# Copies of down-sampled rows issued from ScalarE's queue in two groups, ahead of and behind one block of exponentials

## The chip, the core and the metric

The kernel runs on one core of a Trainium2 chip. The metric is the device time of one execution in microseconds (us). The engines are TensorE (PE; its weight loads are PEld), VectorE (DVE), ScalarE (ACT), GpSimd (POOL) and SyncE (SP), which here only issues transfers. Each engine works through its own instructions in the order in which they were built; a transfer is issued as an instruction of SP, ACT or POOL and lands later by itself, carried by 16 DMA engines that all queues share.

## The reference, cut to what matters

An attention block, and two gated layers behind it. `q`, `k`, `v` have 4 batches, 8 heads, 576 positions and 64 features.

```
q_d, k_d, v_d = means of 4 neighbouring positions          # 144 rows for each head
out_up = repeat(softmax(q_d k_d^T / 8) v_d, 4)             # the down-sampled part
out_local = softmax over |i - j| < 4 of (q k^T / 8) v      # the local part
x = out_up + out_local                                     # 2304 tokens x 512
x = (silu(x w_gate) * (x w_val)) w_out                     # 512 -> 1536 -> 512
out = (h * clip(h + 3, 0, 6) / 6) w2_out,  h = x w2_in     # 512 -> 2048 -> 512
```

All is float32 in accuracy; the inputs come as float64, whose words the kernel decodes itself.

## The kernel before

The 2304 tokens go through the two layers in five blocks (`BLOCKS`, in units of 64 tokens). For every block the weights are brought in pairs of units `w`, split into a high and a low part `wr` (L263 on ACT, L268 on DVE), and multiplied: `pG` (gate) and `pV` (value) of L357, `aO` (output) of L1034, `pH` and `aP` for the second layer. In the first block the weights are decoded from the raw words (`top`, L236 on ACT; `w`, L245 on DVE) and stored in a scratch of the device memory (`kept`, L251, issued by ACT); later blocks read them there. `pG`, `pV` and `pH` use two PSUM banks in turn (`mm`): G0, G1, V0, V1, G2, G3, so G3 writes the bank that V1 wrote, which is free when DVE has multiplied V1 into `sl` (L1004). `gV` is that product, split again (L1009, L1010).

The first batch's attention comes ahead of all this, in `first_batch`, whose steps stand in the string `FRONT`, one word for a step; each engine runs its share of them in this order. The local part works on tiles of 96 positions, i from 0 to 5: `SC` scores, `M` maxima, `W` exponentials (ACT), `N` normalisation (DVE), `PT` transposes into PSUM, `Pa` and `Pd` copies out of it into `turned` (ACT and DVE), `V` the product with the values (`fO` in the traces), `Xh` and `Xl` the result as high and low parts `xr`. `turned` has room for two tiles, so the next `Pa` into the same half waits for the `V` that reads it. The down-sampled part is `dS`, `dM`, `dE`, `dT`, `dP`, `dO`, `dN`; its result lies in `odN`, a piece of a tile named `tmp`. To add it, the values of tile i, `vw[i]`, have 24 more rows under their 102 (WK to KR), and `turned` has ones for them; the step `od` copies 24 rows of `odN` under each of the six tiles by a transfer within the on-chip memory (`join_od`), and `V` of tile i waits for its copy. `de` and `to` decode weights, `hi` and `lo` split them, for the first units.

Two steps concern the second batch: `two` loads two of each four neighbouring positions of its `q` and `k` into staging tiles (`twoq`, `twok`, four transfers on POOL), and `sums` loads the other two on top with an addition (four accumulating transfers), then adds the two that are left (L716, `dnq`, `dnk`, on POOL). The staging tiles belong to a pool that is closed behind `first_batch`; the tiles into which SP loads the second batch's pieces of `q`, `k` and `v` (`load_chunk`, through L141) take their place, so these loads wait for the last sum. With `q` and `k` there, DVE computes the products `pr` (L839) of the second batch between its other work; its place on DVE is the scheduler's choice, as is the place of the transposes `pqT` of the sums (L336) on PE.

Every transfer counts its completion in a semaphore. There are eight for SP and ACT together (DMAHW0 to 7) and eight for POOL (DMASW0 to 7), given out in turn; a transfer whose semaphore another still uses waits for that one.

Of the kernel before, what the change touches and what calls it, by code (L numbers as in the profile page):

```python
# [46 lines left out]
Tq01 Tq00 Eq00 Eq01 Rq0 Tk00 Tk01 Ek01 Tq10 Ek00 Rk0 Tq11 Tk11 dS0 Eq10 Ek11 Eq11 Rq1 Tq20 Tk10 Eq20  # L47
Tk20 Tq21 dM0 Ek10 Ek20 Rk1 dE0 Tq31 Eq21 Tq30 Tk21 Tk31 Eq31 Tk30 dS1 Rq2 Eq30 Ek21 Ek31 Ek30 Rq3
SC0 dM1 M0 Rk3 dE1 Rk2 dT0 dP0 W0 SC1 dS3 dM3 dT1 dP1 SC2 M1 dE3 W1 dS2 dT3 N0 dM2 dP3 SC3 dE2 dT2
PT0 M2 to0 N1 M3 two dP2 to1 de0 Pd0 W3 dO0 dO3 dN0 dN3 dO2 N3 dO1 Pa0 W2 dN2 dN1 od sums to2 PT1  # L50
Pa1 Pd1 SC5 SC4 M5 W5 PT3 V1 M4 N2 Pa3 de1 Xh1 W4 V0 Xh0 Pd3 Xl1 N5 PT2 V3 Pd2 Pa2 Xl0 hi0 PT5 Xh3
N4 Pd5 Pa5 Xl3 to3 V2 Xh2 PT4 de2 Xl2 Pd4 Pa4 de3 V5 lo0 Xh5 V4 Xh4 Xl5 Xl4 hi1 to4 lo1
"""


# [1 line left out]
def tile_kernel(  # L57
# [12 lines left out]
    nc = tc.nc  # L70
# [68 lines left out]
    def late(eng, dst, src):  # L139

        tc.keep_in_program_order(eng.dma_start(dst, src))  # L141
# [172 lines left out]
    def down_sums(b, kinds, gate=None):  # L314
        if gate is not None:
            tc.keep_in_program_order(nc.gpsimd.tensor_copy(consts[:gate.shape[0], 60:61], gate))
        for ws in kinds:
            for t in range(4):
                for w in ws:
                    if t == 0:  # L320
                        dn[w] = sp.tile([NJH, 2, H, D], F32, tag="dn" + w, name=f"dn{w}{b}", bufs=1)
                    src = {"q": q, "k": k, "v": v}[w]
                    for half in range(2):
                        tok = src[b, :, half * NJH * 4:(half + 1) * NJH * 4, :].rearrange("h (j t) d -> j t h d", t=4)
                        how = {"accum_op": ALU.add} if t else {}
                        tc.keep_in_program_order(nc.gpsimd.dma_start(dn[w][:, half], tok[:, t], **how))
                    yield
# [15 lines left out]
    def down_T(b, dn, qk):  # L343
        for w in "qk":
            qk[w] = sp.tile([P, NC, NJ], F32, tag=w + "dT", name=f"{w}dT{b}", bufs=1)
        for w, hc, pt in sums_T(b):
            nc.scalar.activation(qk[w][:, 2 * hc:2 * hc + 2], pt, AF.Copy, scale=1 / 128 if w == "q" else 1.0)
            yield
# [13 lines left out]
    def first_batch():  # L362

        QT = 96
        WK = QT + 6
        KR = WK + QT // 4
# [3 lines left out]
        with tc.tile_pool(name="fp", bufs=1) as fp:  # L370
# [25 lines left out]
            odN = tmp[:NJH, NC * S:NC * S + 2 * DM].rearrange("p (g e) -> p g e", g=2)  # L396
# [53 lines left out]
            vw = []  # L450
# [17 lines left out]

            def join_od(i):
                half, j = divmod(i * QT // 4, NJH)  # L470
                late(nc.gpsimd, vw[i][WK:KR, i % 2], odN[j:j + QT // 4, half])

            for n in range(4):
                load_vd(n)
# [241 lines left out]
                            nc.gpsimd.tensor_tensor(dn[w][:, half], st[:, :, 0], st[:, :, 1], op=ALU.add)  # L716
                        )

            def od():
                for i in (1, 0, 3, 2, 5, 4):  # L720
                    join_od(i)

            def to(i):
# [9 lines left out]
            def lo(i):  # L733
# [4 lines left out]
                "dN": dN, "SC": SC, "M": M, "W": W, "N": N, "PT": PT,  # L738
                "Pa": Pa, "Pd": Pd, "V": V, "Xh": Xh, "Xl": Xl, "sums": sums, "two": two,
                "od": od, "to": to, "de": de, "hi": hi, "lo": lo,  # L740
            }
            for step in FRONT.split():
# [346 lines left out]
    for bi in range(NB):  # L1089
# [29 lines left out]
        sums = iter(())  # L1119
        if db:  # L1120
            sums = down_T(db, dn, qk)
            if bi:
                sums = chain(down_sums(db, ["qk", "v"], state["os"][:, (UMAX // 2 - 2) * DM:][:, :1]), sums)
# [69 lines left out]
```

## Time and profile before

| what | value |
|---|---|
| median of 3 runs | 959.81 us (959.5 to 960.22) |
| profiled execution | 959.29 us |
| its span, first to last instruction | 957.6 us |
| busy in the span | PE 97%, DVE 76%, ACT 53%, POOL 12% |
| TensorE's granted clock, mean | 0.99 |

Busy shares are means over stages that differ: TensorE is full in the blocks and has gaps in the first 80 us, where the first batch's attention runs. What matters there is which wait ended last. In a timeline a row has the start, the duration, the engine, the line, the operation, what it writes and reads, how many instructions it stands for, and in brackets how long the engine had been idle before it and what released it. "issue" in the chain is time in which the engine waited for nothing that the profile shows.

### The profile page before, as it was taken

How to read it: one execution, taken by the hardware profiler on the slowest of the kernel's cores; microseconds unless marked ns; L12 is line 12 of the kernel's file. 1: busy time of each engine (PE TensorE's matmuls, PEld its weight loads, DVE VectorE, ACT ScalarE, POOL GpSimd, SP SyncE). 2: the span in 40 equal slices, each digit the busy share in tenths (PEclk: the TensorE clock that was granted, in tenths of full speed). 3: DMA queues.
4: the chain of work that ended last, by engine and by line, in shares of the span. 5: the costliest groups of instructions: out<-in, count | busy, mean ns of one | idle time of the engine just before them, and what ended most of it. 6: DMA issues, size and time to landing. Idle time of an engine off the chain costs nothing.

```text
span 957.6 us, 13058 instructions
## 1 busy us (share of the span) xinstructions
PE 931.2 (97%) x4848; PEld 789.4 (82%) x4848; DVE 730.4 (76%) x1066; ACT 504.4 (53%) x942; POOL 113.7 (12%) x124
## 2 busy tenths in 40 slices
PE   8799999999899999999999999999999999999997
PEld 5677888777799978878888778888888888999996
DVE  6689967899879979999755799996347994445652
ACT  4785667876444587553334664443335444444542
POOL 7440012000063200015410000000000000000000
PEclk8999999999999999999999999999999999999999
DMA  9899899586699823359962222453223223433331
GB/s 228 178 255 369 294 334 344 166 263 208 236 285 255 159 89 110 130 180 229 216 137 88 67 67 91 165 205 101 97 90 109 89 88 116 148 133 132 120 123 33
DMA packets 100239, 161.08 MB, mean 168 GB/s; under 512 B 53488, under 2 KB 57200, under 8 KB 100176
## 3 DMA queue, kind: packets, MB, share of 16 engines
q1 hardware_dynamic: 57680, 131.43, 42.5%
q0 software_dynamic: 37600, 11.00, 10.6%
q10 hardware_dynamic: 4896, 17.83, 4.7%
q8 instruction: 38, 0.62, 0.3%
q14 instruction: 25, 0.20, 0.1%
HBM read 137.31 MB, written 22.54 MB: 167 GB/s over the span
## 4 chain that ended last, share of the span: by engine, by line
PE 77%; DVE 11%; DMA 4%; issue 3%; ACT 3%; SPq 1%; POOL 0%; ACTq 0%; DVEq 0%
PE aP L1034 17%; PE pH L357 17%; PE aO L1034 13%; PE pG L357 13%; PE pV L357 12%; DVE wr L268 3%; DVE pv L876 1%; DMA vw<-tmp 1%; PE pS L930 1%; SPq L141 1%; DMA w<-in_moe_w_gate_dram 1%; DVE xf L905 1%; DMA kept<-w 1%; PE pO L780 1%; ACT held L153 1%
## 5 line engine op out<-in xcount | busy, mean ns | idle before, releaser
L268 DVE TENSOR_TENSOR wr<-w,wr 128x1024 fp32r<-128x1024 f32 x170 | 207.6, 1222 | 117.9 <-ACT wr L263 117.7
L263 ACT ACTIVATE wr<-w 128x1024 fp32r<-128x1024 f32 x170 | 179.6, 1056 | 127.6 <-issue 61.4
L357 PE MATMUL pH<-x,wr 128*128 128x512 f32 (+1 forms) x960 | 214.0, 373 | 0.0
L1034 PE MATMUL aP<-wr,gH 128*128 128x512 f32 x864 | 212.5, 396 | 0.3 <-ACT gH L1009 0.3
L357 PEld LDWEIGHTS pH<-x,wr 128*128 128x128 f32 x960 | 173.6, 189 | 25.2 <-issue 2.7
L1034 PEld LDWEIGHTS aP<-wr,gH 128*128 128x128 f32 x864 | 159.9, 188 | 35.6 <-issue 2.7
L357 PE MATMUL pG<-xr,wr 128*128 128x512 f32 (+1 forms) x720 | 153.7, 368 | 1.7 <-ACT xr L153 1.2
L357 PE MATMUL pV<-xr,wr 128*128 128x512 f32 (+1 forms) x720 | 153.6, 368 | 0.9 <-ACT sl L998 0.9
L1034 PE MATMUL aO<-gV,wr 128*128 128x512 f32 (+1 forms) x720 | 152.7, 368 | 0.0
L357 PEld LDWEIGHTS pG<-xr,wr 128*128 128x128 f32 x720 | 130.9, 188 | 19.1 <-ACT xr L153 1.4
L357 PEld LDWEIGHTS pV<-xr,wr 128*128 128x128 f32 x720 | 130.9, 188 | 18.1 <-ACT sl L998 1.4
L1034 PEld LDWEIGHTS aO<-gV,wr 128*128 128x128 f32 x720 | 130.8, 188 | 16.7
L1007 ACT ACTIVATE h<-pH,consts 128x512 f32<-128x512 f32 (+1 forms) x80 | 51.5, 643 | 63.1 <-PE pH L357 62.6
L1009 ACT ACTIVATE gV<-sl 128x512 fp32r<-128x512 f32 (+1 forms) x60 | 35.0, 584 | 75.4 <-DVE sl L1004 75.4
L998 ACT ACTIVATE sl<-pG 128x512 f32<-128x512 f32 (+1 forms) x60 | 33.3, 554 | 67.0 <-PE pG L357 66.9
L1009 ACT ACTIVATE gH<-h 128x512 fp32r<-128x512 f32 (+1 forms) x80 | 46.9, 586 | 31.0 <-DVE h L1008 30.8
L839 DVE TENSOR_TENSOR pr<-q,k 128x1792 f32<-128x1792 f32 x27 | 54.6, 2021 | 10.1 <-DMA k<-in_k_dram 9.9
L1008 DVE SCALAR_TENSOR_TENSOR h<-h,pH 128x512 f32<-128x512 f32 (+1 forms) x80 | 50.5, 632 | 14.3 <-ACT h L1007 13.5
L236 ACT ACTIVATE top<-w 128x512 f16<-128x512 bf16 x68 | 52.8, 792 | 13.3 <-DMA w<-in_moe_w_out_dram 4.2
L1010 DVE TENSOR_TENSOR gH<-h,gH 128x512 fp32r<-128x512 f32 (+1 forms) x80 | 50.5, 633 | 11.2 <-ACT gH L1009 10.9
L876 DVE TENSOR_TENSOR pv<-sc,v 128x1792 f32<-128x1792 f32 x27 | 54.6, 2023 | 0.5
L245 DVE SCALAR_TENSOR_TENSOR w<-w,top 128x512 int32<-128x512 int32 x68 | 46.8, 702 | 10.5 <-ACT top L236 7.5
(133 smaller groups left out, 757.9 us busy)
## 6 DMA issues: line engine op xcount, KB each, us to landing
w<-kept SPq DMA_DIRECT2D x136, 512.0 KB
kept<-w ACTq DMA_DIRECT2D x34, 512.0 KB
w<-in_moe_w_out_dram SPq DMA_DIRECT2D x28, 512.0 KB
w<-in_moe_w_in_dram SPq DMA_DIRECT2D x16, 512.0 KB
w<-in_moe_w_gate_dram SPq DMA_DIRECT2D x12, 512.0 KB
w<-in_moe_w_val_dram SPq DMA_DIRECT2D x12, 512.0 KB
out_dram<-os SPq DMA_DIRECT2D x16, 256.0 KB
dnv<-in_v_dram POOLq DMA_DIRECT2D x24, 144.0 KB, 7.7
```

Of the source, the lines that this page charges most:

```text
L236: behind(nc.scalar.activation(halves(top[i % 2], 2, F16)[:, :, 1], h3.bitcast(BF16), AF.Copy))
L245: behind(nc.vector.scalar_tensor_tensor(w32[i // 2][:, i % 2].bitcast(I32), h12, 13, top[i % 2], op0=ALU.logical_shift_right, op1=ALU.bitw ...
L263: behind(nc.scalar.activation(parts[i][:, 0], w32[i // 2].rearrange("p u e -> p (u e)"), AF.Copy))
L268: behind(nc.vector.tensor_tensor(r[:, 1], s, r[:, 0].bitcast(F32), op=ALU.subtract))
L357: nc.tensor.matmul(ps, r[:, a, c], x[:, c, b_, :ps.shape[1]], start=part is HIGH and a == c == 0, stop=part is LOW and c == NC - 1,)
L839: nc.vector.tensor_tensor(pr, qt[:, a:a + SUB, None, :].to_broadcast([P, SUB, W, D]), win(kt, a, SUB), op=ALU.mult)
L876: nc.vector.tensor_tensor(pr, pe[:, a:a + SUB, :, None].to_broadcast([P, SUB, W, D]), win(vt, a, SUB), op=ALU.mult)
L1007: nc.scalar.activation(h, ps, AF.Relu, scale=1 / 6, bias=half1[:, 0:1])
L1008: nc.vector.scalar_tensor_tensor(h, h, 1.0, ps, op0=ALU.min, op1=ALU.mult)
L1009: nc.scalar.activation(g[:, 0, :nt], h, AF.Copy)
L1010: nc.vector.tensor_tensor(g[:, 1, :nt], h, g[:, 0, :nt].bitcast(F32), op=ALU.subtract)
L1034: nc.tensor.matmul(ps, **one, start=f_ == 0 and a == b_ == 0, stop=f_ == nf - 1 and b_ == 1,)
```

## The change

The step `od` becomes two, `od0` (tiles 1 and 0) and `od1` (tiles 3, 2, 5, 4). They stand in `FRONT` behind `M5`, on the two sides of `W5`, where `od` stood behind `dN1` and ahead of `sums`. The six copies are issued by ACT in place of POOL.

```diff
-PT0 M2 to0 N1 M3 two dP2 to1 de0 Pd0 W3 dO0 dO3 dN0 dN3 dO2 N3 dO1 Pa0 W2 dN2 dN1 od sums to2 PT1
-Pa1 Pd1 SC5 SC4 M5 W5 PT3 V1 M4 N2 Pa3 de1 Xh1 W4 V0 Xh0 Pd3 Xl1 N5 PT2 V3 Pd2 Pa2 Xl0 hi0 PT5 Xh3
...
+PT0 M2 to0 N1 M3 two dP2 to1 de0 Pd0 W3 dO0 dO3 dN0 dN3 dO2 N3 dO1 Pa0 W2 dN2 dN1 sums to2 PT1 Pa1
+Pd1 SC5 SC4 M5 od0 W5 od1 PT3 V1 M4 N2 Pa3 de1 Xh1 W4 V0 Xh0 Pd3 Xl1 N5 PT2 V3 Pd2 Pa2 Xl0 hi0 PT5
...
             def join_od(i):
                 half, j = divmod(i * QT // 4, NJH)
-                late(nc.gpsimd, vw[i][WK:KR, i % 2], odN[j:j + QT // 4, half])
+                late(nc.scalar, vw[i][WK:KR, i % 2], odN[j:j + QT // 4, half])
...
-            def od():
-                for i in (1, 0, 3, 2, 5, 4):
+            def od(n):
+                for i in ((1, 0), (3, 2, 5, 4))[n]:
                     join_od(i)
```

On POOL, from the second half of the plain loads on, before (what a row waits for is in brackets):

```order
L703 DMA twok_594<-in_k_dram 72x8x128 [waits DMAHW7_49,DMAHW6_49,PE_49]
L141 DMA vw_261<-tmp 24x512 [waits DVE_49]
L141 DMA vw_261<-tmp 24x512
L141 DMA vw_265<-tmp 24x512 x2
L141 DMA vw_268<-tmp 24x512 [waits DMASW0_49]
L141 DMA vw_268<-tmp 24x512 [waits DMASW1_49]
L703 DMA twoq_588<-in_q_dram 72x8x128 [waits DMASW2_49]
L703 DMA twoq_590<-in_q_dram 72x8x128 [waits DMASW3_49]
L703 DMA twok_592<-in_k_dram 72x8x128 [waits DMASW4_49]
```

and now:

```order
L703 DMA twok_594<-in_k_dram 72x8x128 [waits DMAHW7_49,DMAHW6_49,PE_49]
L703 DMA twoq_588<-in_q_dram 72x8x128 [waits DMASW0_49]
L703 DMA twoq_590<-in_q_dram 72x8x128 [waits DMASW1_49]
L703 DMA twok_592<-in_k_dram 72x8x128 [waits DMASW2_49]
L703 DMA twok_594<-in_k_dram 72x8x128 [waits DMASW3_49]
```

The four plain loads count in DMASW0 to 3. With the copies gone, each accumulating load waits for the plain load into the same tile; before, it waited for the load or copy that had the semaphore last.

On DVE, in the first block behind the first decodings, before (`sl_0`, `sl_1` belong to V0 and V1, `wr_999` to the weights of V2 and V3, `pr` to the second batch):

```order
L245 SCALAR_TENSOR_TENSOR w_8_1023<-w_8_884,top_159 128x512
L1010 TENSOR_TENSOR gV_0_991<-sl_0_942,gV_0_991 128x512
L1004 TENSOR_TENSOR sl_1_964<-sl_1_964,pV_1_1002 128x512
L268 TENSOR_TENSOR wr_999<-w_6_970,wr_999 128x1024
L839 TENSOR_TENSOR pr_0_0_1092<-q_0_972,k_0_974 128x1792
L1010 TENSOR_TENSOR gV_1_1015<-sl_1_964,gV_1_1015 128x512
L245 SCALAR_TENSOR_TENSOR w_8_1023<-w_9_890,top_161 128x512
```

and now:

```order
L839 TENSOR_TENSOR pr_0_0_1092<-q_0_972,k_0_974 128x1792
L1010 TENSOR_TENSOR gV_0_991<-sl_0_942,gV_0_991 128x512
L268 TENSOR_TENSOR wr_999<-w_6_970,wr_999 128x1024
L1004 TENSOR_TENSOR sl_1_964<-sl_1_964,pV_1_1002 128x512
L245 SCALAR_TENSOR_TENSOR w_8_1023<-w_9_890,top_161 128x512
L245 SCALAR_TENSOR_TENSOR w_10_1066<-w_10_967,top_159 128x512
```

`pr` stands ahead of `gV_0`, `wr_999` and `sl_1` in place of behind them.

On PE, in the first block from the second `pV` on, now (`pG_3` is the fourth `pG`, G3):

```order
L357 MATMUL pV_1_1002<-xr_786,wr_918 128x512 x11
L357 MATMUL pG_2_1025<-xr_786,wr_948 128x512 [waits DVE_49]
L357 MATMUL pG_2_1025<-xr_786,wr_948 128x512 x11
L336 MATMUL pqT_0_1162<-ident,dnq_684 128x72 [waits PE_49,Pool_49]
L336 MATMUL pqT_0_1162<-ident,dnq_684 128x72 [waits Pool_49]
L336 MATMUL pqT_0_1162<-ident,dnq_684 128x72 x2
L357 MATMUL pG_3_1047<-xr_786,wr_948 128x512 [waits DVE_49]
```

The order of the products is as before; the first transposes `pqT` have come from behind the first `aO` to between `pG_2` and `pG_3`.

## Rows read from the trace of the kernel before

**Rows 1.** The chain of waits: start (us), duration (us), what held it.
```profile
10.07 4.72 DMA fnk<-in_k_dram
...
37.91 9.59 DMA vw<-tmp
...
120.57 5.44 PE pG L357 x24
```

**Rows 2.** TensorE's timeline, from the last stage of the first batch on.
```profile
45.79 1.55 PE L153 MATMUL fO<-turned,vw 126*64 126x96 f32 x16 [5.78 <-DMA vw<-tmp]
...
57.77 5.78 PE L357 MATMUL pG<-xr,wr 128*128 128x512 f32 x24 [1.24 <-ACT xr L153]
...
68.83 5.60 PE L357 MATMUL pG<-xr,wr 128*128 128x512 f32 x24
...
78.08 3.03 PE L357 MATMUL pV<-xr,wr 128*128 128x512 f32 x12 [0.94 <-ACT sl L998]
```

**Rows 3.** ScalarE's timeline; ACTq is an issue of a transfer.
```profile
37.44 0.67 ACT L153 ACTIVATE turned<-fPT 102x384 f32<-102x384 f32 x1
38.41 0.34 ACT L153 ACTIVATE held<-fS,fnm 96x102 f32<-96x102 f32 x1 [0.30 <-DVE fnm L153]
...
46.81 0.49 ACT L153 ACTIVATE turned<-fPT 102x384 f32<-102x384 f32 x1 [5.69 <-PE fO L153]
...
56.80 0.33 ACTq L251 DMA_DIRECT2D kept<-w  x1
57.26 0.46 ACT L153 ACTIVATE xr<-fO 128x384 fp32r<-128x384 f32 x1
```

**Rows 4.** GpSimd's timeline.
```profile
30.76 1.87 POOL L703 DMA_DIRECT2D twoq<-in_q_dram  x2 [0.52 <-issue]
...
37.37 3.09 POOL L141 DMA_DIRECT2D vw<-tmp  x6 [3.14 <-DVE tmp L153]
43.30 1.45 POOL L703 DMA_DIRECT2D twoq<-in_q_dram  x1 [2.83 <-DMA twok<-in_k_dram]
45.12 1.40 POOL L703 DMA_DIRECT2D twoq<-in_q_dram  x1 [0.38 <-DMA twok<-in_k_dram]
46.03 3.29 POOL L703 DMA_DIRECT2D twok<-in_k_dram  x2
55.60 5.46 POOL L716 TENSOR_TENSOR dnq<-twoq 72x512 f32<-72x512 f32 x2 [6.28 <-DMA twoq<-in_q_dram]
63.95 3.07 POOL L716 TENSOR_TENSOR dnk<-twok 72x512 f32<-72x512 f32 x2 [2.88 <-DMA twok<-in_k_dram]
```

**Rows 5.** SyncE's issues of the second batch's first loads.
```profile
67.04 0.33 SPq L141 DMA_DIRECT2D q<-in_q_dram  x1
67.42 0.42 SPq L141 DMA_DIRECT2D k<-in_k_dram  x1
```

**Rows 6.** VectorE's timeline about `pr`.
```profile
73.22 2.02 DVE L839 TENSOR_TENSOR pr<-q,k 128x1792 f32<-128x1792 f32 x1 [2.38 <-DMA k<-in_k_dram]
75.17 0.69 DVE L1010 TENSOR_TENSOR gV<-sl,gV 128x512 fp32r<-128x512 f32 x1
...
78.90 1.22 DVE L268 TENSOR_TENSOR wr<-w,wr 128x1024 fp32r<-128x1024 f32 x1
80.04 0.68 DVE L1004 TENSOR_TENSOR sl<-sl,pV 128x512 f32<-128x512 f32 x1
```

**Rows 7.** What the tile `twoq` shows: its four transfers' time to landing.
```profile
DMA to landing us min/median/max: 6.5/10.1/12.3
```

**Rows 8.** Busy time by stretch: engines, then TensorE's granted clock, DMA share, GB/s.
```profile
33.00:57.00 24.00, 17.49 (x228) 15.03 (x226) 16.43 (x39) 16.43 (x72) 11.37 (x13) 0.86 1.16 211
57.00:63.00 6.00, 5.23 (x23) 4.30 (x24) 5.70 (x8) 5.59 (x8) 4.07 (x2) 1.00 1.02 337
63.00:66.00 3.00, 3.00 (x15) 2.49 (x14) 1.40 (x2) 2.26 (x4) 2.05 (x2) 1.00 0.53 105
45.80:50.60 4.80, 4.60 (x41) 3.89 (x42) 2.61 (x5) 3.70 (x19) 3.53 (x3) 0.50 1.11 251
```

More of the change, by code (lines that the diff above doesn't have):

```diff
@@ L49 @@
 SC0 dM1 M0 Rk3 dE1 Rk2 dT0 dP0 W0 SC1 dS3 dM3 dT1 dP1 SC2 M1 dE3 W1 dS2 dT3 N0 dM2 dP3 SC3 dE2 dT2
-PT0 M2 to0 N1 M3 two dP2 to1 de0 Pd0 W3 dO0 dO3 dN0 dN3 dO2 N3 dO1 Pa0 W2 dN2 dN1 od sums to2 PT1
-Pa1 Pd1 SC5 SC4 M5 W5 PT3 V1 M4 N2 Pa3 de1 Xh1 W4 V0 Xh0 Pd3 Xl1 N5 PT2 V3 Pd2 Pa2 Xl0 hi0 PT5 Xh3
-N4 Pd5 Pa5 Xl3 to3 V2 Xh2 PT4 de2 Xl2 Pd4 Pa4 de3 V5 lo0 Xh5 V4 Xh4 Xl5 Xl4 hi1 to4 lo1
+PT0 M2 to0 N1 M3 two dP2 to1 de0 Pd0 W3 dO0 dO3 dN0 dN3 dO2 N3 dO1 Pa0 W2 dN2 dN1 sums to2 PT1 Pa1
+Pd1 SC5 SC4 M5 od0 W5 od1 PT3 V1 M4 N2 Pa3 de1 Xh1 W4 V0 Xh0 Pd3 Xl1 N5 PT2 V3 Pd2 Pa2 Xl0 hi0 PT5
+Xh3 N4 Pd5 Pa5 Xl3 to3 V2 Xh2 PT4 de2 Xl2 Pd4 Pa4 de3 V5 lo0 Xh5 V4 Xh4 Xl5 Xl4 hi1 to4 lo1
 """
```

## The prediction

> **What bounds the kernel now.** I read the chain of waits first, since it names the work that sets the end. From about 78 us on it holds matmuls of TensorE almost without a gap, a run of 24 taking 5.44 us [rows 1], so the time is set by when TensorE comes through the stages before that, and an edit in the first batch is worth what it moves there. The chain names one long link in the first batch, 9.59 us of the copies `vw<-tmp` [rows 1]. TensorE's timeline shows what that link costs: a stop of 5.78 us before the first `fO`, whose matmuls read the copied rows, then the first `pG` at 57.77, the second pair of `pG` at 68.83, and one more small stop, 0.94 us, before the half pair of `pV` at 78.08 [rows 2]. The reader should compare this with the DVE rows, because that second stop has a cause that the change touches: DVE stood 2.38 us until the load of `k` landed and ran `pr` at 73.22 only then [rows 6]. SP's rows tell why `k` came so late: `q` and `k` are issued at 67.04 and 67.42 [rows 5], right behind the last sum `dnk` on GpSimd (63.95 + 3.07 = 67.02), which had itself waited for the load of `twok` [rows 4]. So there are two chains in the first 80 us: copies, `fO`, `pG`; and sums, `q` and `k`, `pr`.
>
> **The copies.** Six copy issues leave GpSimd and six come to ScalarE. Before, the first stands at 37.37, when the last normalisation is done, and the six issues take 3.09 us [rows 4]. Their landing takes 9.59 us [rows 1], although each has only 48 KB, because they stand in one queue behind four loads of 288 KB, of which POOL still saw one land at 43.30 [rows 4]. On ScalarE two copies come between `turned` (37.44) and the exponentials (38.41) [rows 3]. An issue on that queue takes 0.33 us [rows 3], so two cost 0.7 us, of which the 0.30 us that ScalarE waits there now is hidden; the exponentials start about 0.3 us late. Nobody waits for them early, and ScalarE next stands idle 5.69 us [rows 3], which takes in the four later issues (1.3 us) as well.
>
> How soon a copy lands on ScalarE's queue no row shows. Bounds: 4.72 us for a load of 144 KB on SP's queue while the DMA engines were busy [rows 1], and the 9.59 us of now. I take 4, near the first, because nothing else stands in ScalarE's queue then: `fO` starts at about 42 in place of 45.79. From the next `turned` (46.81) to the last `xr` (57.26) ScalarE's stream decides the start of `pG` [rows 3], and it moves by about 4.4 us: first `pG` at 53.4. Half a pair is 2.72 us, so TensorE, after the five halves of `pG`, `pG`, `pV`, `pV`, `pG`, would come to its fourth `pG` at 53.4 + 13.6 + 0.2 for the transposes now placed there = 67.2, against 68.83 + 2.72 = 71.55 now.
>
> **The order on DVE.** Here the gain is lost. The order of the built program (the pieces shown with the change) has `pr` two places further ahead, before `gV_0`, `wr_999` and `sl_1`. `sl_1` is what empties the PSUM bank that the fourth `pG` writes, and TensorE's row there waits for DVE. Engines work in order, so the fourth `pG` now waits for `k`. From the start of `pr` to the end of `sl_1`: 1.95 for `pr` (73.22 to 75.17), 0.69 for `gV`, 1.14 for `wr` (78.90 to 80.04), 0.68 for `sl`, together 4.46 us [rows 6]. Before, `sl_1` and `wr_999` came first and only `gV_1` and a decoding stood behind the late `pr`, hence a stop of no more than 0.94 us.
>
> If `pr` starts at 73.22 as now, the fourth `pG` starts at 77.7, after a stop of 10.5 us, and the half pair of `pV` now at 78.08 starts 5.44 later, at 83.1: 5.0 us late. Each microsecond by which `pr` starts earlier gives one back; the break-even is `pr` at 68.2. Behind it DVE has done no less than before, so I cost the rest at nothing: TensorE's stream covers it.
>
> **When k lands.** GpSimd goes from the first four loads straight to the four accumulating ones. In the order its first accumulate waited for the completion count DMASW2, that of the first `twok` load, since with six copies between them the counts were used up; now it waits for DMASW0, that of its own first load. So the first two move from 43.30 and 45.12 to about 37.3 and 41 (30.76 plus the shortest landing, 6.5 [rows 7]). The `twok` ones still need the plain `twok` loads, seen landed at 43.30 and 45.12, so they move from 46.03 and about 47.7 to 43.0 and about 45: some 3 us.
>
> Does the landing move with them? The DMA engines are the answer: their share is 1.16 from 33 to 57, 1.02 from 57 to 63, and falls to 0.53 only from 63 to 66 [rows 8], when the sums' last load lands. Full engines finish the same bytes at the same time whatever the order within. What comes 4 us earlier with the new timeline (two stores to `kept`, two weight loads, 512 KB each) fills the place that the early accumulates leave. So I keep the landing at 63.95 and later, the sums' end at 67.02 and `pr` at 73.22. Bounds: 3.0 us earlier (by issue alone), or 6.2 (all of the copies' place in that queue, from 43.30, when a plain `twok` load had landed, to the last copy's landing, issued at about 39.9 and 9.6 later: 49.5), or 3.1 later (below).
>
> **The clock.** The row of 45.8 to 50.6 has a granted clock of 0.50, the lower level of 1.2 GHz, behind a stop of 5.78 us [rows 2, 8]; 4.8 us at half the clock cost 2.4 us of matmuls. The new stop is longer, and the slow stretch may lie inside it. Bounds 0 and 2.4; I take 1.2.
>
> **Sum.** 5.0 + 1.2 = 6.2 us. The profiled execution took 959.29 us (its span and 1.7 around it), 0.5 under the median 959.81. 959.3 + 6.2 = 965.5 us, slower.
>
> **Rivals.**
> - *The sums land early enough* (the other side). Place: GpSimd's queue between 43 and 57 us. The copies are gone from it and the accumulates no longer wait for a foreign count. If that brings `dnk` 5 us or more ahead, `pr` starts before 68.2 and the change is faster; at 62.7 or before, TensorE doesn't stop at all, and the gain is 4.4 + 0.94 = 5.3 us: 954. Between: 954 to 957.4. For it: the place of 6.2 us that comes free in that queue, and the 6.28 us for which GpSimd waited before `dnq` [rows 4]. Against: the full DMA engines. Chance 0.18; and 0.10 that it comes out near the break-even, within 0.2% (1.9 us, about what a measurement here can tell from no change).
> - *The sums move by their issue alone*, 3.0 us: 5.0 - 3.0 = 2.0, with about 1 for the clock 962.3. Chance 0.09.
> - *The sums land later.* Each of their packets waits behind those of other loads, and one weight load and one `kept` store that now come after the sums' landing move in front of it: 1.05 MB, at 337 GB/s [rows 8] 3.1 us. 6.2 + 3.1 = 9.3: 968.6. Chance 0.12. This is what the Trainium skill, "DMA: Bandwidth & Descriptors", section "Queues, rings and completion order", would make of it: a DMA engine takes turns among its queues, a packet at a time, which favours large packets over the sums' small ones. No row here tells the turns.
> - *The change doesn't do what it says*: the copies land as late from ScalarE's queue. Then `pG` stays at 57.8, but the fourth `pG` still waits for `k` to 77.7, after a stop of 6 us: 5.0, with 1.2 for the clock 965.5 again. Chance 0.06. The Trainium skill speaks for it (same page, "Issuing engines are not separate DMA queues": all queues share the same 16 engines, so another issuer saves only issue time). The trace agrees on the shared load, but the 9.59 us stand behind loads of the same queue.
> - The forecast itself: 0.45, its own range 963 to 968.
>
> **Numbers.** Slower by over 0.2%: 0.45 + 0.09 + 0.12 + 0.06 = 0.72; within: 0.10; faster: 0.18. The range goes from 957, which leaves out most of the fastest case, to 970, for later sums with the whole of the clock's price.
>
> **What would show it.** Copies: `fO` starts at 41 to 43 with a stop of 1 to 3 us. ScalarE: `pG` begins at 52.5 to 54.5. DVE: idle 8 us or more before `pr`, released by the load of `k`, `pr` at 72 to 76. TensorE: its longest stop of the first 100 us lies before the fourth `pG`, released by DVE. The step is wrong if `pr` starts before 69: then the sums' landing moved, and with it the forecast's sign.

## The result, and the profile after

The changed kernel took 968.41 us (median of 4 executions, 965.29 to 970.41), the kernel before 959.72 beside it: a ratio of 1.0087, 95% interval 1.0059 to 1.0114. On a second chip the same two took 965.91 (9 executions, 963.76 to 971.98) and 961.02 (32, 959.06 to 966.37): 1.0055, 1.0032 to 1.0077. The change makes the kernel 5 to 9 us slower. The forecast was 965.5, range 957 to 970. The profiled execution took 965.29, 6.0 more than that of the kernel before.

The chain of waits (start, duration, what held it) no longer names the copies [rows 1], but the accumulating load of `twoq`, GpSimd's additions, and the load of `k`:

```profile
40.21 15.60 DMA twoq<-in_q_dram
...
55.88 4.08 POOL dnq L716
...
65.95 6.77 DMA k<-in_k_dram
...
76.70 0.61 DVE sl L1004
...
77.35 3.02 PE pG L357 x12
```

So the chain now runs through `k` to `pr` (72.94), `gV`, `wr` and `sl` on VectorE, and from there to the fourth `pG`. TensorE's timeline shows the price:

```profile
46.27 2.83 PE L153 MATMUL fO<-turned,vw 126*64 126x96 f32 x32 [5.13 <-DMA vw<-tmp]
...
58.40 2.10 PE L357 MATMUL pG<-xr,wr 128*128 128x512 f32 x8 [1.24 <-ACT xr L153]
...
73.80 0.42 PE L336 MATMUL pqT<-ident,dnq 72*128 72x72 f32 x4
77.35 3.02 PE L357 MATMUL pG<-xr,wr 128*128 128x512 f32 x12 [3.14 <-DVE sl L1004]
80.21 5.60 PE L357 MATMUL pV<-xr,wr 128*128 128x512 f32 x24
```

Against [rows 2]: the first `fO` is no earlier (46.27, 45.79 before), the first `pG` 0.63 later, and the fourth `pG`, which followed the third at once, waits 3.14 for `sl`. The half pair of `pV` that stood at 78.08 starts at 80.21 + 2.72 = 82.93, 4.85 late.

VectorE's rows against [rows 6]: `pr` starts at 72.94 (73.22 before), released by `k` as there, but `sl` is now behind it. The first row is for a later point.

```profile
58.74 1.76 DVE L245 SCALAR_TENSOR_TENSOR w<-w,top 128x512 int32<-128x512 int32 x1
...
69.15 0.69 DVE L245 SCALAR_TENSOR_TENSOR w<-w,top 128x512 int32<-128x512 int32 x1
72.94 2.02 DVE L839 TENSOR_TENSOR pr<-q,k 128x1792 f32<-128x1792 f32 x1 [3.10 <-DMA k<-in_k_dram]
74.88 0.68 DVE L1010 TENSOR_TENSOR gV<-sl,gV 128x512 fp32r<-128x512 f32 x1
75.48 1.22 DVE L268 TENSOR_TENSOR wr<-w,wr 128x1024 fp32r<-128x1024 f32 x1
76.62 0.68 DVE L1004 TENSOR_TENSOR sl<-sl,pV 128x512 f32<-128x512 f32 x1
```

ScalarE issues the copies, and waits for `fO` nearly as long as before (4.86, 5.69 in [rows 3]):

```profile
38.08 2.10 ACTq L141 DMA_DIRECT2D vw<-tmp  x2
40.23 0.34 ACT L153 ACTIVATE held<-fS,fnm 96x102 f32<-96x102 f32 x1 [1.78 <-DVE fnm L153]
```

GpSimd's timeline, against [rows 4], and SyncE's issues, against [rows 5]:

```profile
37.94 1.41 POOL L703 DMA_DIRECT2D twoq<-in_q_dram  x1 [3.33 <-DMA twoq<-in_q_dram]
40.21 1.39 POOL L703 DMA_DIRECT2D twoq<-in_q_dram  x1 [0.85 <-DMA twoq<-in_q_dram]
43.44 2.77 POOL L703 DMA_DIRECT2D twok<-in_k_dram  x2 [1.84 <-DMA twok<-in_k_dram]
51.51 1.27 POOL L716 TENSOR_TENSOR dnq<-twoq 72x512 f32<-72x512 f32 x1 [5.30 <-DMA twoq<-in_q_dram]
55.88 4.08 POOL L716 TENSOR_TENSOR dnq<-twoq 72x512 f32<-72x512 f32 x1 [3.09 <-DMA twoq<-in_q_dram]
59.91 5.63 POOL L716 TENSOR_TENSOR dnk<-twok 72x512 f32<-72x512 f32 x2
```

```profile
64.44 0.38 SPq L219 DMA_DIRECT2D w<-in_moe_w_gate_dram  x1
65.57 0.33 SPq L141 DMA_DIRECT2D q<-in_q_dram  x1
65.95 1.01 SPq L141 DMA_DIRECT2D k<-in_k_dram  x1
```

The accumulating loads are issued at 37.94, 40.21 and 43.44 (43.30, 45.12 and 46.03 before), and GpSimd's last two additions (`dnk`) wait for no load any more: they start when the one before them ends, 4 us before the 63.95 at which `dnk` began before. But the last three additions take 9.7 us without a gap, and of these `dnk`'s two take 5.63, where they took 3.07. They end at 65.54, before at 67.02, and `k` lands about half a microsecond earlier than it did.

### The profile page after: what moved, and what is told of

It is laid out like the page before. It is cut to its first block, busy times and chain, and to the rows that moved or that the text cites. A ratio compares the mean times of both kernels' runs of the same rounds, so it can differ in the third digit from the quotient of the medians.

```text
span 963.6 us, 13049 instructions
## 1 busy us (share of the span) xinstructions
PE 933.8 (97%) x4848; PEld 792.1 (82%) x4848; DVE 731.6 (76%) x1066; ACT 504.0 (52%) x942; POOL 112.0 (12%) x118
## 3 DMA queue, kind: packets, MB, share of 16 engines
q10 hardware_dynamic: 5112, 18.12, 4.7%
## 4 chain that ended last, share of the span: by engine, by line
PE 75%; DVE 10%; DMA 6%; issue 4%; POOL 2%; ACT 1%; SPq 1%; DVEq 0%; POOLq 0%; ACTq 0%
PE pH L357 18%; PE aP L1034 17%; PE aO L1034 13%; PE pV L357 12%; PE pG L357 12%; DVE wr L268 3%; DMA twoq<-in_q_dram 2%; DMA k<-in_k_dram 1%; DVE pv L876 1%; SPq L141 1%; PE pS L930 1%; DMA w<-in_moe_w_in_dram 1%; PE pO L780 1%; DVE xf L905 1%; DVE sc L842 1%
```

## The experiments

A *stop* is idle time of TensorE. Each kernel ran beside the kernel before; the table gives its ratio to that, taken over all executions, so it can differ from the ratio of the two medians:

| run | what it is | median us | ratio, 95% interval |
|---|---|---|---|
| e1_after_again | the changed kernel | 965.91 | 1.0055 (1.0032 to 1.0077) |
| e2_pr_behind | it, `pr` behind `sl_1` | 962.34 | 1.0008 (0.9989 to 1.0027) |
| e3_pr_ahead | kernel before, `pr` ahead of `sl_1` | 962.81 | 1.0022 (1.0004 to 1.0040) |
| e4_sp_first | copies on SyncE ahead of three weight loads | 958.26 | 0.9971 (0.9954 to 0.9988) |
| e5_sp_first_pr_late | e4, `pr` behind `gV_2` | 961.42 | 1.0005 (0.9987 to 1.0023) |
| e6_pr_late | changed kernel, `pr` behind `gV_2` | 964.07 | 1.0036 (1.0018 to 1.0054) |
| e7_two_late | e6, plain loads behind the copies | 969.29 | 1.0071 (1.0046 to 1.0095) |
| e8_pool_od_first | copies on GpSimd ahead of its plain loads | 965.29 | 1.0035 (1.0015 to 1.0054) |
| e9_act_old_place | kernel before, copies issued by ScalarE | 969.33 | 1.0074 (1.0045 to 1.0102) |
| e10_pr_behind_gv1 | e4, `pr` behind `gV_1` | 958.97 | 0.9991 (0.9966 to 1.0016) |
| e11_weights_ahead | e8, two weight loads ahead of `q` | 963.21 | 1.0018 (0.9997 to 1.0038) |
| e12_sp_first_again | e4 again | 959.21 | 0.9981 (0.9959 to 1.0002) |

**e1, the changed kernel again.**

> The changed kernel once more, unaltered, to see how far its executions spread (965.3 to 970.4 in four) and to have a second profile. Theory A (the loss is VectorE's order: pr stands ahead of sl_1 and waits for k): 965 to 970 with the fourth pG starting 4.4 us behind pr wherever k lands, so a longer execution has a later k. Rival R (the loss lies in later stretches, in the granted clock or the weights): the stop before the fourth pG is the same 3 us in a longer execution, and the rest differs.

Its profile (965.91) has another shape than the first one:

```profile
32.85 7.87 PE L153 MATMUL fdO<-fvd,fdpT 72*72 72x65 f32 x64
...
78.52 3.03 PE L357 MATMUL pG<-xr,wr 128*128 128x512 f32 x12 [0.93 <-DVE sl L1004]
```

From 30 to 40 us its granted clock is 0.50, the lower level, where in the first profile it was 0.85 up to 35 us and 1.00 behind that; the 64 matmuls of `fdO`, which take 4.47 at the higher level, take 7.87. TensorE comes late to everything: the copies are issued from 42.3, the first `pG` starts at 61.78, and the wait behind `pr` (74.10) is down to 0.93. So the fourth `pG` starts 4.42 behind `pr`, as theory A has it (4.41 in the first profile), and the total is the same by another way: two chains end there, and the later one counts. e12's profiled execution (967.92, its others 957.04 to 961.23) has the slow `fdO` too, with 7.88. It is not what makes the changed kernel slow in general: the mean granted clock over the span is 0.983 in this execution of e1 and 0.986 to 0.991 in the eight others, which take 963.76 to 971.98.

**e2, the order on VectorE taken back.** An edge of order keeps `pr` behind `sl_1`; nothing waits longer for its data.

```diff
-                nc.vector.tensor_tensor(h, h, ps, op=ALU.mult)
+                mul = nc.vector.tensor_tensor(h, h, ps, op=ALU.mult)
+                if bi == 0 and f == 1:
+                    state["mul1"] = mul.ins
...
+            with tc.issue_after(state.pop("mul1")) if "mul1" in state else ExitStack():
```

> The changed kernel with one edge of order added on VectorE: pr may not be issued before sl_1. Theory A: the stop of 3.1 us before the fourth pG goes, the half pair of pV comes 4 to 5 us earlier than 83.0, and the time is 959 to 962, about that of the kernel before, since the copies land no earlier than there. Rival R: 965 or more, as without the edge.

962.34 beside 961.02: the loss of 0.55% is gone but for 0.08%, and the interval includes a ratio of 1. The profile has the third and fourth `pG` in one row, and `pr` behind `sl`:

```profile
71.57 5.60 PE L357 MATMUL pG<-xr,wr 128*128 128x512 f32 x24
```

```profile
72.00 0.68 DVE L1005 TENSOR_TENSOR sl<-sl,pV 128x512 f32<-128x512 f32 x1
72.88 2.02 DVE L840 TENSOR_TENSOR pr<-q,k 128x1792 f32<-128x1792 f32 x1 [0.20 <-DMA k<-in_k_dram]
```

`pr` starts at the same time as without the edge. Theory A holds: the loss is the place of `pr` on VectorE. Two sizes missed: the median is 0.3 above the range expected, and the half pair of `pV` comes 3.2 us earlier (79.73 in place of 82.93), not 4 to 5. The edge also sent the transposes `pqT`, 0.42 us of TensorE, back behind the first `aO`; no run separates the two, but their size is a tenth of what came back.

**e3, that order alone in the kernel before.** `pr` is traced within V0 and tied: behind `sl_0`, with `gV_0` and `sl_1` behind it.

```diff
+                with tc.issue_after(state["pr1"]) if bi == 0 and f == 1 else ExitStack():
+                    mul = nc.vector.tensor_tensor(h, h, ps, op=ALU.mult)
+                if bi == 0 and f == 0:
+                    state["mul0"] = mul.ins
+                    next(state["first"])
```

> The kernel before (copies still issued by GpSimd in one group) with VectorE's order alone altered: pr stands behind sl_0 and ahead of gV_0 and sl_1. pr started at 73.22 there; pr, gV and sl are 3.3 us, so the fourth pG starts at about 76.6 in place of 71.55. Theory A: +4 us and up to 1.2 for the clock, 963.5 to 965. Rival R (it takes the changed issue of the copies): 959.5 to 960.5.

+1.8 us by the medians, half of what A gave and below its range; the interval excludes a ratio of 1, which is the rival's, by 0.04% only. The profile tells why it is less: here the wait for `sl` has come to stand before the next pair,

```profile
73.65 3.02 PE L357 MATMUL pG<-xr,wr 128*128 128x512 f32 x12 [0.43 <-ACT sl L1002]
78.91 7.34 PE L357 MATMUL pV<-xr,wr 128*128 128x512 f32 x24 [2.24 <-DVE sl L1009]
```

since in this build the fourth `pG` took the bank that the third had left, and V2 the one that `sl_1` frees. It isn't quite the same edit, then: it has the direction of A, and the order's size rests on e2.

**e9, the issuing engine alone.** One line: `nc.scalar` for `nc.gpsimd`, the copies at their old place in one group.

> The kernel before with only the issuing engine changed: the six copies from ScalarE, in one group at their old place in FRONT (ahead of sums). In the order of the built program pr stands ahead of gV_0, wr_999 and sl_1 already with this one edit. Theory A: as slow as the changed kernel, +3 to +7 us against the kernel before (964 to 968 where that is 961), so the two groups around W5 have no part in the loss. Rival R (the place around W5 counts, the engine doesn't): within 1.5 us of the kernel before.

+8.65 us, more than the whole change. `pr` stands ahead of `sl_1` here too, so this one line brings the order. But the sixth copy could be issued only at 45.6, behind the landing of an earlier transfer whose completion count it takes over (by the trace a copy; which one isn't shown), and on ScalarE everything else stood behind that issue:

```profile
37.09 9.24 ACTq L141 DMA_DIRECT2D vw<-tmp  x6
46.44 0.78 ACT L236 ACTIVATE top<-w 128x512 f16<-128x512 bf16 x1 [9.54 <-DMA vw<-tmp]
```

The exponentials of tile 5 and `turned` of tile 1 come behind it, and the first `fO` starts at 49.82. So what was expected was wrong in giving the two groups no part: with the first pair ahead of `W5`, `fO` starts at 46.27. They save some of what the queue costs. The time of e9 is therefore the order's price and the queue's together.

**e4 and e12, the copies on another queue.** The six copies are issued by SyncE, in one group, and the weight loads 4 to 6 behind them (parts of lines):

```diff
-                late(nc.scalar, vw[i][WK:KR, i % 2], odN[j:j + QT // 4, half])
+                late(nc.sync, vw[i][WK:KR, i % 2], odN[j:j + QT // 4, half])
...
-dN2 dN1 sums to2 PT1 Pa1
-Pd1 SC5 SC4 M5 od0 W5 od1 PT3
+dN2 dN1 od0 od1 lr sums to2 PT1 Pa1
+Pd1 SC5 SC4 M5 W5 PT3
```

> The six copies issued by SyncE's queue in one group, with the loads of raw weights 4 to 6 behind them in that queue (they are ahead of the copies in time in the changed kernel, 33.5 to 35.8 against 38.1); VectorE has pr behind sl_1 as before. Theory B (the copies landed late because those three loads of 512 KB were ahead of them on the way that SyncE's and ScalarE's transfers share): the first two copies land within 3.5 us of issue, the first fO starts at 41 to 43 in place of 46.3, and the time is 955 to 957.5. Rival B' (the DMA engines are full with GpSimd's loads): landing 6 to 7 us after issue as now, fO at 45 or later, 959 to 962.

> e4_sp_first once more, unaltered, beside e10: 956 to 962 with a median 2 to 3 us under the kernel before. If the gain was chance of the first series, within 1 us of it.

The time is 2.8 us under the kernel before, in the second series 1.5. That is near the number of theory B, but not for its reason: the first `fO` starts at 45.31, so the copies land as late (issued from 37.5) with no weight load ahead of them. B falls, and B' holds for the copies. VectorE keeps the order of the kernel before, and the first `pG` is 1.16 earlier than there (in a profiled execution of 961.75, one of the two longest of twelve):

```profile
45.31 2.83 PE L153 MATMUL fO<-turned,vw 126*64 126x96 f32 x32 [5.00 <-DMA vw<-tmp]
...
56.61 5.76 PE L357 MATMUL pG<-xr,wr 128*128 128x512 f32 x24 [1.24 <-ACT xr L153]
```

**e5, e6, e10: how far back `pr` may go.** The edge of e2, behind `gV_2` (e5, e6) or `gV_1` (e10).

```diff
+            if bi == 0 and f == 2 and kind == "V":
+                state["low2"] = low.ins
...
+            with tc.issue_after(state.pop("low2")) if "low2" in state else ExitStack():
```

> e4_sp_first with pr behind gV_2 on VectorE (two half pairs later), so that no product of the first block stands behind k. Theory A (what was left of the loss in e4 is VectorE waiting for k: 4.1 us, and a stop of 3.4 us before the second half pair of pV): the stop goes, and the time falls by 2 to 4.5 us under e4's 958.3, to 954 to 956. Rival (that stop hides other waits, for weights that land late): under 1 us less, 957.5 or more.

> The changed kernel with pr behind gV_2 on VectorE. Theory A: like e2 or better, no stop of TensorE over 1.7 us from the first pG on, 959.5 to 962. It is also the base for the next run, which has the same order on VectorE.

> e4_sp_first with pr behind gV_1 on VectorE, one step later than there (e5 had it behind gV_2). Theory A: the stop of 3.4 us before V3 goes, as in e5, and pr isn't late enough to give it back at the end of the block's first layer: 1 to 3 us faster than e4, run again beside it. Rival (pr anywhere behind sl_1 costs the same sum, only at another place): within 1 us of e4.

The stops in the first products go each time, and the time doesn't follow: e5 is no faster than e4 (1.0005 against 0.9971, and 0.9981 when e4 ran again), e6 no faster than e2 (1.0036 against 1.0008), e10 as fast as e12 beside it. Whether e5 and e6 are slower isn't settled, since these intervals overlap. In e6 what was saved comes back at the end of the first layer, where VectorE's postponed work stands ahead of what `pH` needs:

```profile
163.96 3.03 PE L357 MATMUL pH<-x,wr 128*128 128x512 f32 x11 [1.86 <-ACT x L1050]
```

This shows one stop of 1.86 in one execution; whether it is the whole difference wasn't settled.

**e7 and e8: why the copies land late.** e7 holds GpSimd's four plain loads until the copy of tile 0 has landed, with the copies still on ScalarE; e8 is the kernel before with GpSimd's copies ahead of its plain loads. Both have `pr` behind `gV_2`, so e7 differs from e6 by the loads alone. Parts of e7's lines:

```diff
-nc.gpsimd.tensor_copy(consts[:QT, 60:61], nm[3][:QT, 0, :1])
+nc.gpsimd.tensor_copy(consts[96:KR, 60:61], vw[0][96:KR, 0, :1])
...
-M3 two dP2
+M3 dP2
...
-od1 PT3
+od1 two sums PT3
```

> e6_pr_late with GpSimd's four plain loads of twoq and twok held until the copy of tile 0 has landed; the copies are still issued by ScalarE and the weight loads still ahead of them. Theory C (the copies land late because GpSimd's plain loads, in packets of 4096 bytes, slow the loads of v in packets of 256 bytes ahead of them): the copies land within 4 us of issue, the first fO starts at 41 to 43, the first pG at 53 to 54.5, and the time is 954 to 957, or up to 5 more if the later sums make k later than gV_2 (k at 80 or after). Rival D (the copies are slow by themselves on ScalarE's queue, or behind the raw weight loads): landing 6 us or more after issue, fO at 45 or later.

> The kernel before with GpSimd's copies issued ahead of its four plain loads, so that nothing stands ahead of them in its queue, and pr behind gV_2. Theory C: the copies land within 4 us of issue from GpSimd as well, fO at 41 to 43: the issuing engine isn't what counts. 954 to 957, or up to 5 more with a late k. Rival D: landing 6 us or more, fO at 45 or later, 958 or more.

e7, then e8:

```profile
42.46 2.83 PE L153 MATMUL fO<-turned,vw 126*64 126x96 f32 x32 [2.96 <-DMA vw<-tmp]
...
53.84 5.73 PE L357 MATMUL pG<-xr,wr 128*128 128x512 f32 x24 [1.24 <-ACT xr L153]
```

```profile
41.40 2.13 PE L153 MATMUL fO<-turned,vw 126*64 126x96 f32 x32 [2.14 <-DMA vw<-tmp]
...
52.47 5.73 PE L357 MATMUL pG<-xr,wr 128*128 128x512 f32 x24 [1.24 <-ACT xr L153]
```

Theory C holds for the copies: with the plain loads out of the way the first are there by 42.5 and 41.4, from ScalarE's queue as from GpSimd's, and the first `pG` starts 4 to 5 us earlier than before. The queues of the DMA engines from 34 to 38 us (packets, MB, share of the 16 engines) show how, first the changed kernel, then e7:

```profile
q0 software_dynamic: 234, 0.68, 84.7%
q1 hardware_dynamic: 388, 0.10, 15.2%
```

```profile
q1 hardware_dynamic: 1382, 0.82, 78.7%
```

q0 is GpSimd's queue with the plain loads, q1 SyncE's with the last loads of `v` and then the weights. Beside GpSimd's loads SyncE's queue gets 388 packets through in 4 us, alone 1382. By the Trainium skill ("DMA: Bandwidth & Descriptors", section "Queues, rings and completion order") a DMA engine takes turns among its queues, a packet at a time. The trace agrees in direction: the queue with small packets (0.26 KB each, by the row) gets far fewer bytes than the one with large ones (2.9 KB). It does not show turns of one packet each, with 388 packets to 234, nor that the profile counts packets as the Trainium skill does.

The copies themselves did not lose such turns. ScalarE's queue is q10: over the execution it carries 18.12 MB, the 34 stores `kept` and the six copies. In the changed kernel the first copy is issued at 38.08, and from 38 to 43.6 us q10 has no packet at all, while the two other queues go on:

```profile
q1 hardware_dynamic: 938, 0.89, 68.6%
q0 software_dynamic: 161, 0.40, 38.7%
```

In e7 the first copy is issued at 36.59, and q10 has none until 40.2, while q1 alone takes 97% of the engines. So the copies had not begun. Whether they stood behind SyncE's transfers in a path common to both queues, no run settles.

The totals are another matter: +8.9 and +4.9 us by the medians, where at most 962 was expected. In both the sums come later, SyncE issues `q` at 72.81 and 71.34 with `k` right behind, and the weight loads 11 and on stand behind them. TensorE stops for 8.67 us in e7, before the second half pair of `pV`, and VectorE has nothing to decode for 8.61 us in e8:

```profile
81.01 0.69 DVE L245 SCALAR_TENSOR_TENSOR w<-w,top 128x512 int32<-128x512 int32 x1 [8.61 <-ACT top L236]
```

**e11, the weights ahead of `q`.** e8 with `load_chunk` two units later in SyncE's order (`CLOAD = (4, 6)` for `(2, 6)`), `pr` behind `gV_3`.

> e8_pool_od_first with the weight loads 11 and 12 ahead of the loads of q, k and v in SyncE's queue, and pr behind gV_3, two steps later in the program. Theory E (what ate the early copies' gain of 5.3 us in e8 is SyncE's queue: the loads of q, k and v wait there for the late sums and hold back the weights, so VectorE and ScalarE stood 8.6 us for them): the stops of 4.5 us between 80 and 95 go, 3 to 6 us less than e8 (which was 4.9 over the kernel before). Rival (the DMA engines are what is late, whatever the order): within 1.5 us of e8.

+2.5 us where e8 had +4.9: less than the 3 to 6 us that were expected, and with overlapping intervals. The wait has moved on to the loads that are still behind `q`:

```profile
85.88 0.69 DVE L245 SCALAR_TENSOR_TENSOR w<-w,top 128x512 int32<-128x512 int32 x1 [7.43 <-ACT top L236]
```

SyncE's queue is at most part of the price. Of the versions tried, only e4 (with its repetition e12) and e10 have medians under the kernel before, and only e4's first interval excludes a ratio of 1; a part of its gain may be chance (the second ends at 1.0002).

## Why the prediction was right, and where not

- **The order on DVE: right, and it is the loss.** From the start of `pr` to the end of `sl_1` I had 4.46 us; measured, from `pr` to the fourth `pG`, 4.41 and 4.42. Forecast were the fourth `pG` at 77.7 and the half pair of `pV` at 83.1; they came at 77.35 and 82.93. e2 takes the loss away with this order (and the small move of `pqT`), and e9 shows that the issuing engine alone brings the order about.
- **The copies: wrong.** I took 4 us from issue to landing because nothing stood in ScalarE's queue, and `fO` at about 42. `fO` started at 46.27; the rival that the copies land as late, which I gave 0.06, is what happened. The first two issues took 2.10 us in place of 0.7, and the exponentials started at 40.23, 1.8 later than before; nobody waited for them. The number didn't suffer: `pG` had only to be in time for `pr`. In place of a stop of 10.5 us there is one of 3.14, with the same end. That is also why this rival had the forecast's time. Of the signs named, `pr` between 72 and 76 and a stop released by DVE came; the times of `fO` and `pG`, an idle time of 8 us before `pr` (3.10) and the longest stop at the fourth `pG` (it is still the 5.13 before `fO`) did not.
- **The landing of `k`: right by luck.** "Full engines finish the same bytes at the same time whatever the order within" failed in this execution. Before, `dnk` waited for its load until 63.95; now GpSimd had its loads by 59.9 at the latest. The DMA share of 57 to 63 fell from 1.02 [rows 8] to 0.82, and from 63 to 66 from 0.53 to 0.21:

```profile
57.00:63.00 6.00, 4.24 (x21) 3.06 (x18) 6.00 (x9) 3.79 (x6) 6.00 (x2) 1.00 0.82 289
63.00:66.00 3.00, 2.46 (x11) 1.76 (x10) 3.00 (x2) 2.97 (x4) 2.54 (x2) 1.00 0.21 36
65.00:80.00 15.00, 11.37 (x52) 9.28 (x53) 10.67 (x12) 7.87 (x12) 0.55 (x1) 1.00 0.85 293
```

  What kept `k` late here is a step that I had not priced: the additions. One took 1.27 at 51.51, the next 4.08, and all three last ones together 9.7. In the 6.00 us of the first of these rows VectorE (third of the busy times) was busy for 6.00, and GpSimd (fifth) too. VectorE was slowed as well: its `w` of 0.69 took 1.76 at 58.74. By the Trainium skill ("SBUF — State Buffer", section "Who interferes with whom") the two engines share one pair of ports to the on-chip memory under an exclusive lock, and a VectorE instruction with two inputs there contends with a GpSimd instruction that reads it. The durations fit that; no run here took VectorE's work away from beside the additions, so it isn't shown as the cause.

  Two other profiles with the same transfers end in other waits. In e1 the additions are over at 61.66 (57.63 + 4.03), and SyncE issues `q` only behind a weight load, which waited for VectorE:

```profile
66.71 0.38 SPq L219 DMA_DIRECT2D w<-in_moe_w_gate_dram  x1
67.52 0.33 SPq L141 DMA_DIRECT2D q<-in_q_dram  x1
```

  In the first profile that weight load came at 64.44 and `q` at 65.57, so shorter additions alone would have brought `q` forward by about 0.75 us (an estimate from these rows: 65.57 - 64.44 - 0.38). In e2 the sums' last load lands as late as before:

```profile
64.37 1.49 POOL L716 TENSOR_TENSOR dnk<-twok 72x512 f32<-72x512 f32 x1 [1.74 <-DMA twok<-in_k_dram]
```

  With three different last waits `pr` starts at 72.94, 74.10 and 72.88. That the forecast had 73.22 is luck.
- **The clock: not in this execution.** I added 1.2 us for a slow stretch behind the new stop. There was none: the row of 65 to 80 has a granted clock of 1.00, with TensorE idle for 3.6 of the 15 us. But other runs have the stretch that I meant. In e4's profile the granted clock is 0.50 behind a stop of 3.42, and a half pair takes 4.43 in place of 3.03, 1.4 us more:

```profile
79.39 4.43 PE L357 MATMUL pV<-xr,wr 128*128 128x512 f32 x12 [3.42 <-ACT sl L1002]
```

```profile
79.40:82.40 3.00, 3.00 (x7) 2.42 (x8) 3.00 (x4) 1.58 (x3) 0.00 (x0) 0.50 0.77 227
```

  e3's profile has it behind its stop of 2.24, where the pair of `pV` takes 7.34. So the size was near; whether the stretch comes differs between profiles. That the profiled time of the changed kernel comes out at +6.0 without it is due to small later stops, the largest that the kernel before does not have being this one:

```profile
150.75 3.01 PE L357 MATMUL pV<-xr,wr 128*128 128x512 f32 x12 [1.34 <-ACT sl L998]
```

- **The spread was not foreseen.** Three of the first four executions took 968 to 970 and so lie above the forecast's own range of 963 to 968. No profile of one was taken. Their mean granted clock, 0.988, 0.986 and 0.990, is no lower than the 0.986 of the profiled execution, so a lower clock does not tell them apart from it. On the other chips the kernel before also ranges over 7 to 8 us. What the slowest executions lose, and where, stays open.

## What to carry to other kernels

Where a scheduler places the instructions, read the order of the built program on the engines that wait: one changed issue moved `pr` ahead of `sl_1`, and that, not the transfer that the change was about, was the loss: about 4 us by e2, about 2 by e3's less exact edit. Before a transfer is given to another queue, look at what the DMA engines carry at that time: from two other queues the first `fO` came within half a microsecond of where it was (46.27 and 45.31; e9 is 4 us later), and from either of two it came 3 to 4 us earlier once GpSimd's large loads were not under way. And a wait that is taken away is worth only what the next chain leaves: here that of the sums, `k` and the weights behind it in one queue took back all of it and more in e7 and e8.

## What the runs showed of the hardware that was not expected

- Two DMA queues do not share the engines by bytes: SyncE's moved 0.10 MB (388 packets) in 4 us beside 0.68 MB of GpSimd's, and 0.82 MB (1382 packets) without them.
- A transfer on a queue that is otherwise empty can wait for its first packet: 5.5 us on ScalarE's queue in the changed kernel and 3.6 in e7, with the engines busy for other queues.
- The same addition on GpSimd, 72 x 512, took from 1.27 to 4.08 us. VectorE was busy all the time beside the shortest as well (1.27 of 1.27 us from 51.51, 4.07 of 4.07 from 55.88), so its busy share does not tell them apart; beside the short one it ran a copy `turned`, a part of `xr` and a small operation on `fsm`, beside the long one decodings `w` and a split `wr` too.
- A stop of much the same length is followed by the lower clock or not: 0.50 behind 3.42 us in e4, 1.00 behind 3.14 in the changed kernel.
- Executions of one kernel differ by when TensorE is at the lower clock. At 0.50 from 30 to 40 us the 64 matmuls of `fdO` took 7.87 us in place of 4.47. From 20 to 30 us TensorE had been busy for 8.68 us in that execution and for 8.89 in the other.
